# Attention of a mixed kernel: chunks of 64 tokens, two sequences in the halves of the partitions, state carried from pair to pair

## The chip, the core and the metric

The kernel runs on one core of one Trainium2 chip. A core has a matrix engine (TensorE, PE in the profile, with the loading of its weights shown as PEld), a vector engine (VectorE, DVE), an activation engine (ScalarE, ACT), a general engine (GpSimd, POOL) and a queue that issues most transfers (SyncE, SP). Data lie in an on-chip memory of 128 partitions; PE writes to eight banks of its own accumulation memory, 128 partitions by 512 numbers of 32 bits each, and ACT and DVE read them out. The metric is the time of one execution in microseconds (us). All numbers are 32-bit floats.

## The reference

Two blocks in a row. The first is a chunked state-space attention over 4 sequences, 8 heads, 768 tokens, head width 32 and state width 16. The chunk length is free to choose, since the chunked form gives the same numbers for any length:

```python
cum = np.cumsum(la, axis=-1)                    # la = log of the decays a, in one chunk
L = np.exp(cum[:, :, :, None] - cum[:, :, None, :]) * causal
M = np.einsum('bhin,bhjn->bhij', Cc, Bc) * L
y = einsum('bhij,bhjd->bhid', M, xc) + einsum('bhin,bhnd->bhid', Cc, state) * np.exp(cum)
state = exp(sum(la)) * state + sum over j of (Bc[j] x xc[j]) * np.exp(cum[-1] - cum[j])
```

Its output, 3072 tokens of 256 numbers, goes through the second block: four branches e with two layers each, weighted by normalized probabilities p:

```python
for e in range(4):                              # w1: 256 x 1024, w2: 1024 x 256
    out += p[:, e:e+1] * (np.maximum(x @ w1[e], 0.0) @ w2[e])
```

## The kernel before, in words

**The branches.** Tokens are taken in four blocks of 768; a block has three pairs of 256 columns (`yT`, one value of kind V per pair, features in the partitions and tokens in the columns). The matrix products of both layers are made by a fast scheme of sums and products (20 products instead of 24 per group of four feature blocks); each product is `product` (L1017), two matmuls of 128x128 weights with 256 columns, and stands in the trace as four records. DVE and POOL make the sums of weights (L1077), of tokens (L1147) and of results (L1044, L1357), DVE the gates (L1052), and ACT moves banks to memory and back (L1026, L1031, L1317). Weight sums of the first block are stored and read again by the later blocks.

**The attention before.** A chunk is 128 tokens of one sequence; chunks go round the four sequences, so that chunk c follows on chunk c - 4. For each chunk:

- transfers (`fetch`): the tokens and heads `xb`; the running sums of the log decays, spread over all partitions, `ab` (512 KB); the same sums per head, `ah`.
- `decays`: the matrix L of each head in `MT`, 128x128. It is made by ACT (`decay`, eight exponentials per chunk, L525) and cut to the causal half by POOL (`causal`, L535), or, in the first chunks and in chunks 2 and 4 (`SCANS`), by DVE as a scan along the columns (`scan`, L518) into a buffer of its own, `LT0`. `fade` (L544, L885) puts B times the last column of L beside it, as 16 more columns of MT.
- `score` (L501): four matmuls of 32 rows, 128 columns of weights and 256 columns. DVE multiplies the result into MT (L940).
- `outputs`: the carried state times the query, four matmuls on 32x32 pieces of the array (L963), where neighbouring chunks turn the output by some quarters of the partitions; and `inner` (L550), eight matmuls of 128 rows, 32 columns of weights and 144 columns: 128 for the output and 16 for the new state.
- `carry`: ACT takes the 16 columns out (L560), DVE transposes them and adds the old state times its decay (L994, L996).

Two chunks are a pair of 256 columns. Scores are made for two chunks in a burst, outputs for two or four.

**What sets the order.** Up to about 13 us the instructions stand as written (the opening): loads, identity and masks, logs and their sums by PE (`sum_logs`), probabilities (`turn_gates`, `spread_gate`), chunks 0 and 1 with decays by the scan (`spread` on PE, L665, then `scan`), and half of the first product (`first_half`, L697). Everything after goes through a planner (`Plan`): PE's order is the list `line`; the other engines' work is placed by due times that follow from it, with durations and a start time written into the code. Buffers of each kind are given out by it. `PAIRS_AT` says at which step of which unit the scores and outputs of the next block's chunks enter the list. SP issues the transfers in the planner's order. The end of the last block (`last`) turns results with PE (L1431), copies them out and stores each with one transfer (`send`, L1435); the blocks before it store through `leave` (L1411).

The kernel names its planned costs; those that the change touches, as they are before:

```python
pe(.66 * len(cs), lambda e: score(
pe(.93 + .49 * len(cs) if cs[0] >= NSEQ else .4 + .49 * len(cs), fn, reads=reads, ...
now, START = 13.0, 12.1
```

Of the kernel before, what the change touches and what calls it, by code (L numbers as in the profile page):

```python
# [35 lines left out]
SCORED, OWN, LEAD, LEFT = 7, 4, 5, 3  # L36
SCANS = 2, 4
FILLED, EARLY, FADE = 3, 4, "POOL"
CUT = {(c, 0): "DVE" for c in range(2, 6)}
HORIZON, OPENING, LOADED = 26.0, 80.0, 0.5  # L40
ORDERS = (0, 1, 2, 3), (3, 1, 2, 0), (0, 1, 2, 3), (3, 1, 2, 0)
PAIRS_AT = ((1, 22, "s0"), (2, 1, "o0"), (2, 1, "s1"), (2, 24, "s2"), (3, 0, "o12")), (
    (1, 1, "s0"), (1, 24, "s1"), (2, 0, "o01"), (2, 24, "s2"), (3, 1, "o2"))
# [316 lines left out]
def kernel(  # L360
# [17 lines left out]
    HN = P  # L378
    T = NCH * P
    OB, OBT, OCT = DM, DM + HN, DM + 2 * HN  # L380
# [6 lines left out]
    SPREAD = 3  # L387
# [3 lines left out]
    assert NSEQ == E == EPB == 4 and sum(b.n for b in blocks) == NCH  # L391

    def real(c):
        return c % NSEQ * NC + c // NSEQ

    def turn_of(c):

        return (0, 2, 1, 3)[c % NSEQ]

    def turned(c):  # L400

        lo = P // NQ * turn_of(c) if c >= NSEQ else 0
        return [(lo, 0, P - lo), (0, P - lo, lo)][:1 + (lo > 0)]
# [5 lines left out]
    acut_d = tc.dram_tile([NCH, NH, P], FP32, name="acut_d")  # L409
    cum_d = tc.dram_tile([NCH, NH, P], FP32, name="cum_d")  # L410
    p_d = tc.dram_tile([E, NCH, P], FP32, name="p_d")
# [9 lines left out]
    def some(n, shape, name, pool=const):  # L421
# [3 lines left out]
        "V": some(NV - 4, [P, 2, FB], "v"),  # L425
        "W": some(NW, [P, 2 * FB], "w"),
        "bank": some(8, [P, 512], "bank", psum),
        "xb": some(4, [P, W], "xb"),
        "ab": some(4, [P, NH * P], "ab"),
        "ah": some(3, [HN, P], "ah"),  # L430
        "MT": some(2, [P, 2, NH, P + N], "MT"),
        "ctm": some(4, [HN, NT, P], "ctm"),
        "cts": some(4, [HN, NT, P], "cts"),
        "dec": some(8, [HN, P], "dec"),
        "A": some(4, [P, NT, N], "A"),
        "S": some(10, [HN, D], "S"),
        "gate": some(2, [P, max(b.n for b in blocks), P], "gate"),
        "Y": some(12, [P, FB], "Y"),
        "cum": some(2, [NCH * NH // 2, 2, P], "cum"),
        "neg": some(1, [P, 2, NCH * NH // 2], "neg"),  # L440
        "dram": [None, None, None],
    }
    LT0 = const.tile([P, 2, NH, P], FP32, name="LT0")
    homes["V"][:0] = [
        LT0[:, j, h:h + NQ].rearrange("p (a h) s -> p a (h s)", a=2)
        for j in range(2) for h in range(0, NH, NQ)]
    st = {c: {} for c in range(NCH)}
# [4 lines left out]
    def load_tokens(c, xb):  # L452
        src = xbc[real(c)]
        if len(turned(c)) > 1:
            nc.sync.dma_start(out=xb[:, :OBT], in_=src[:, :OBT])
            for there, here, n in turned(c):
                nc.sync.dma_start(out=xb[here:here + n, OBT:], in_=src[there:there + n, OBT:])
        else:
            nc.sync.dma_start(out=xb, in_=src)

    def load_decays(c, ab):
        nc.sync.dma_start(
            out=ab, in_=(acut_d if c in SCANS else cum_d)[real(c)].rearrange("h s -> (h s)").partition_broadcast(P))

    def load_heads(c, ah):
        src = cum_d[real(c)].unsqueeze(1).to_broadcast([NH, N, P])
        for there, here, n in turned(c):
            nc.sync.dma_start(out=ah[here:here + n], in_=src[there // N:(there + n) // N])
# [23 lines left out]
    def mask(c, ctm, xb):  # L492
        for t in range(NT):
            nc.scalar.mul(ctm[:, t], xb[:, OCT:OCT + P], tmask[:, t:t + 1])  # L494

    def score(cs, ctm, xb, banks, order=range(4)):
        views = [b.rearrange("p (c t s) -> p c t s", c=2, t=NT) for b in banks]
        for j, c in enumerate(cs):
            for r in order:
                k = slice(32 * r, 32 * r + 32)  # L500
                nc.tensor.matmul(  # L501
                    out=views[r][:, j], lhsT=xb[j][k, OBT:OBT + P],
                    rhs=ctm[j][k].rearrange("p t s -> p (t s)"),
                    start=(j == 0), stop=True, tile_position=(32 * r, 0),
                    skip_group_check=True)

    def quarter(c, r):

        q = (r + (turn_of(c - c % 2) if c >= NSEQ else 0)) % NQ
        return slice(NT * q, NT * q + NT)  # L510

    def place(c, h):

        return (h + NH // 2) % NH if c >= NSEQ and c % 2 else h

    def scan(LT, src, lo):
        w = src.shape[1]
        nc.vector.tensor_tensor_scan(  # L518
            out=LT.rearrange("p h s -> p (h s)")[:, lo:lo + w], data0=src,
            data1=ident.rearrange("p h s -> p (h s)")[:, :w], initial=0.0,  # L520
            op0=ALU.mult, op1=ALU.add)

    def decay(c, MT, ab, neg, h):

        nc.scalar.activation(  # L525
            out=MT[:, place(c, h), 0:P], in_=ab[:, h * P:h * P + P], func=AF.Exp,
            bias=neg[:, h % NT, NQ * real(c) + h // NT:NQ * real(c) + h // NT + 1])

    def causal(e, MT, h, n):
        if e == "DVE":  # L530
            nc.vector.tensor_tensor(
                out=MT[:, h:h + n, 0:P], in0=MT[:, h:h + n, 0:P],
# [1026 lines left out]
    for c in (4, 5):  # L1559
        carry(c)  # L1560
# [152 lines left out]
```

## Time and profile before

| | us |
|---|---|
| median of 3 runs | 609.67 (609.55 to 609.75) |
| the profiled execution's own time | 609.86 |
| its span, first to last instruction | 608.1 |
| PE busy | 602.0 |
| DVE busy | 490.5 |
| ACT busy | 296.0 |
| POOL busy | 159.3 |
| transfers | 99.78 MB, 164 GB/s over the span |
| granted clock of PE | 1.00 |

A group of the profile is one line of the code on one engine with one shape. For a matmul, `32*128 32x256` means weights of 32 rows and 128 columns, and 256 columns streamed over 32 rows. The busy time of a group does not count the overlap with the instruction before it, so a mean of 380 ns with a busy time of 384.3 us for 1636 records is no contradiction: records overlap. `<-` names what ended the idle time before a group. In a timeline the first column is the start, the second the time from the first start to the last end of the merged instructions.

### The profile page before, as it was taken

What the parts mean: (1) busy time and instruction counts of PE and PEld (TensorE: products, weight loads), DVE (VectorE), ACT (ScalarE), POOL (GpSimd) and SP (SyncE); (2) the same over time, 40 slices, a digit from 0 to 9 for tenths busy, and PEclk for the clock granted to TensorE, in tenths of its full rate; (3) what the DMA queues carried; (4) which work ended last, traced back from release to release, by engine and by line L of the source; (5) the groups of instructions that cost most, each with busy time, mean ns of one, the idle gap of its engine ahead of it and who ended that gap; (6) DMA issues with size and microseconds to landing.
All of it is one profiled execution on the core that took longest, in us unless ns stands there. A gap on an engine that the chain in (4) does not pass through costs nothing.

```text
span 608.1 us, 10074 instructions
## 1 busy us (share of the span) xinstructions
PE 602.0 (99%) x3381; PEld 515.1 (85%) x3381; DVE 490.5 (81%) x842; ACT 296.0 (49%) x698; POOL 159.3 (26%) x208
## 2 busy tenths in 40 slices
PE   8999999999999999999999999999999999999997
PEld 5778878888888888888888888888888888888886
DVE  7779999999989894777879988396785989576695
ACT  5567475488443328948251334734444242434441
POOL 7565664646451002776400100200000000000000
PEclk9999999999999999999999999999999999999999
DMA  7968569786924239982432324962241322974001
GB/s 219 280 202 270 164 208 329 258 286 218 319 83 116 61 71 330 286 288 106 138 96 87 113 33 144 326 199 90 70 138 63 110 72 35 331 227 143 1 0 53
DMA packets 88564, 99.78 MB, mean 164 GB/s; under 512 B 26932, under 2 KB 54208, under 8 KB 88512
## 3 DMA queue, kind: packets, MB, share of 16 engines
q1 hardware_dynamic: 88356, 99.08, 52.3%
q8 instruction: 27, 0.44, 0.3%
q14 instruction: 25, 0.20, 0.1%
q10 hardware_dynamic: 156, 0.06, 0.0%
HBM read 78.93 MB, written 20.17 MB: 163 GB/s over the span
## 4 chain that ended last, share of the span: by engine, by line
PE 97%; DVE 1%; DMA 0%; ACT 0%; issue 0%; SPq 0%; DVEq 0%
PE bank L1017 91%; PE bank L550 2%; PE bank L501 2%; PE bank L963 1%; PE bank L690 1%; PE bank L665 0%; DMA w<-in_w_dram 0%; DVE bank L1175 0%; PE bank L1494 0%; DVE v L1044 0%; PE bank L1431 0%; DVE v L1052 0%; ACT A L560 0%; PE bank L697 0%; PE bank L655 0%
## 5 line engine op out<-in xcount | busy, mean ns | idle before, releaser
L1017 PE MATMUL bank<-v,w 128*128 128x256 f32 x1636 | 384.3, 380 | 0.3 <-DVE v L1044 0.2
L1017 PEld LDWEIGHTS bank<-v,w 128*128 128x128 f32 x1636 | 309.4, 190 | 45.8 <-issue 2.2
L1017 PE MATMUL bank<-Y,w 128*128 128x256 f32 x692 | 177.1, 381 | 0.6 <-ACT LT L978 0.4
L1317 ACT COPY v<-bank 128x512 f32<-128x512 f32 x105 | 61.5, 586 | 184.4 <-PE bank L1017 183.0
L1017 PEld LDWEIGHTS bank<-Y,w 128*128 128x128 f32 x692 | 130.6, 190 | 21.1 <-ACT v L1026 0.9
L1044 DVE TENSOR_TENSOR v<-v,v 128x512 f32<-128x512 f32 x183 | 136.3, 760 | 2.3 <-ACT v L1026 0.9
L1052 DVE SCALAR_TENSOR_TENSOR v<-bank,gate 128x512 f32<-128x512 f32 x145 | 99.5, 687 | 43.6 <-PE bank L1017 40.4
L1077 POOL TENSOR_TENSOR w<-w,w 128x512 f32<-128x512 f32 (+1 forms) x77 | 84.7, 1109 | 49.5 <-DVE v L1044 19.2
L1175 DVE TENSOR_TENSOR bank<-bank,v 128x512 f32<-128x512 f32 x82 | 55.9, 695 | 34.5 <-PE bank L1017 17.9
L1026 ACT COPY v<-bank 128x512 f32<-128x512 f32 x99 | 58.0, 586 | 49.0 <-PE bank L1017 39.0
L1031 ACT COPY bank<-v 128x512 f32<-128x512 f32 x122 | 70.5, 592 | 9.0 <-DVE v L1052 3.9
L1017 PE MATMUL bank<-LT,w 128*128 128x256 f32 x232 | 58.4, 380 | 0.0
L525 ACT ACTIVATE MT<-ab,neg 128x128 f32<-128x128 f32 x160 | 50.6, 392 | 4.9 <-DMA ab<-cum_d 4.9
L1017 PEld LDWEIGHTS bank<-LT,w 128*128 128x128 f32 x232 | 43.9, 190 | 6.4 <-issue 0.6
L535 POOL TENSOR_SCALAR_AFFINE_SELECT MT<-MT 128x512 f32<-128x512 f32 x38 | 24.6, 653 | 74.5 <-ACT MT L525 54.6
L1044 DVE TENSOR_TENSOR v<-bank,v 128x512 f32<-128x512 f32 x27 | 18.6, 688 | 9.0 <-PE bank L1017 7.4
L1357 DVE TENSOR_TENSOR v<-v,v 128x256 f32<-128x256 f32 x63 | 24.0, 420 | 0.9 <-ACT v L1317 0.7
L940 DVE TENSOR_TENSOR MT<-bank,MT 128x512 f32<-128x512 f32 x36 | 22.8, 682 | 1.6 <-POOL w L1077 1.2
L1044 POOL TENSOR_TENSOR v<-v,v 128x512 f32<-128x512 f32 x7 | 8.9, 1272 | 44.3 <-DVE v L1044 44.3
L1052 DVE SCALAR_TENSOR_TENSOR v<-v,gate 128x512 f32<-128x512 f32 x27 | 19.2, 710 | 0.4
L1317 ACT COPY LT<-bank 128x512 f32<-128x512 f32 x15 | 8.8, 584 | 17.2 <-PE bank L1017 17.2
L494 ACT ACTIVATE ctm<-xb,tmask 128x128 f32<-128x128 f32 x48 | 15.9, 390 | 1.0 <-DMA xb<-in_xbc_dram 0.9
(121 smaller groups left out, 322.9 us busy)
## 6 DMA issues: line engine op xcount, KB each, us to landing
w<-w_d SPq DMA_DIRECT2D x128, 256.0 KB
w<-in_w_dram SPq DMA_DIRECT2D x72, 256.0 KB
w_d<-w SPq DMA_DIRECT2D x64, 256.0 KB
ab<-cum_d SPq DMA_DIRECT2D x20, 512.0 KB
gate<-p_d SPq DMA_DIRECT2D x15, 384.0 KB
xb<-in_xbc_dram SPq DMA_DIRECT2D x17, 192.0 KB
out_dram<-v SPq DMA_DIRECT2D x144, 16.0 KB
xb<-in_xbc_dram SPq DMA_DIRECT2D x7, 320.0 KB
```

The source lines that it names most:

```text
L525: nc.scalar.activation(out=MT[:, place(c, h), 0:P], in_=ab[:, h * P:h * P + P], func=AF.Exp, bias=neg[:, h % NT, NQ * real(c) + h // NT:NQ ...
L535: nc.gpsimd.affine_select(out=MT[:, h:h + n, 0:P], in_=MT[:, h:h + n, 0:P], compare_op=ALU.is_ge, fill=0.0, base=0, pattern=[[0, n], [1, P ...
L940: nc.vector.tensor_mul(to, g, to)
L1017: nc.tensor.matmul(out=o, lhsT=w[:, j], rhs=x if half is None else x[:, j], start=(start and j == 0), stop=(j == 1), skip_group_check=True)
L1026: act(.5, lambda e: nc.scalar.copy(out=flat(v), in_=bank.t), reads=[bank], writes=[v])
L1031: act(.54 if to - lo > FB else .32, lambda e: nc.scalar.copy(out=bank.t[:, lo:to], in_=flat(v)[:, lo:to]), reads=[v], writes=[bank])
L1044: plan.add(engines, lambda e: (on(e).tensor_add if sign > 0 else on(e).tensor_sub)(flat(v), whole(x), whole(y)), reads=[x, y], writes=[v], ...
L1052: dve(D512, lambda e: nc.vector.scalar_tensor_tensor(out=h.t, in0=whole(x).rearrange("p (j m) -> p j m", j=JJ), scalar=0.0, in1=g.t[:, 2 * ...
L1077: (on(e).tensor_add if sign > 0 else on(e).tensor_sub)(out, x, y)
L1175: dve(D512, lambda e: (nc.vector.tensor_add if sign > 0 else nc.vector.tensor_sub)(to.t, bank.t, whole(x)), reads=[x, bank], writes=[to])
L1317: act(.5, lambda e: nc.scalar.copy(out=flat(v), in_=bank.t), reads=[bank], writes=[v], hold=HOLD)
L1357: plan.add(engines, lambda e: (on(e).tensor_add if sign > 0 else on(e).tensor_sub)(o[1](), x[1](), y[1]()), reads=[v for v in vs if v is n ...
```

## The change

A chunk becomes 64 tokens. A pair is now the 64-token chunks of all four sequences at the same place, 256 columns as before, so there are twelve pairs, and pair p follows on pair p - 1. Sequences 0 and 1 lie in partitions 0 to 63 of the decay matrices, 2 and 3 in 64 to 127; s is the half, c the place within it, z = 2s + c the sequence.

- L per head and sequence is 64x64; `MT` is 128 x (4, 2, 2, 64). `decay` makes 16 exponentials of 64 columns per pair, `causal` is DVE's minimum with a bound, over 512 columns, twice per pair; pairs 0 and 1 use the scan. `LT0`, `SCANS`, `CUT`, `FADE` and `acut_d` are gone.
- `score`: sixteen matmuls per pair, 32 rows, 64 columns of weights, 128 columns. `scores` takes one pair or two.
- `outputs`: sixteen matmuls of state times query (32x32, 128 columns), 32 of `inner` (64 rows, 32 columns of weights, 64 columns), and sixteen of a new function `state` (64 rows, 32 columns of weights, 64 columns) with the decayed B in a buffer `F` of its own. The new state comes out with its rows in place, so DVE's transpose goes; `carry` takes the two heads of a quarter with masks.
- `unturn` takes the second half's output back to its quarters with ACT.
- Transfers: tokens `xt` (two per pair), heads `bct` (one per two pairs, 512 KB), `ab` in four issues and 512 KB per pair, `ah` in four issues per pair from a second copy of the sums, `cumh_d`.
- The opening makes pair 0 (one set of four scans, one inner stage) and the spread of pair 1; the first product is left to the planner. All four first weights are loaded ahead of pair 1's tokens.
- `leave` and `last` store by the new order of tokens; a `send` of `last` is two transfers, one per half of the partitions.
- `PAIRS_AT` and the planner's costs are written for the pairs.

In the built program PE has 2263 matmuls in place of 1698, DVE 851 instructions for 842, ACT 641 for 699, POOL 141 for 208, SP 559 for 548.

```diff
-PAIRS_AT = ((1, 22, "s0"), (2, 1, "o0"), (2, 1, "s1"), (2, 24, "s2"), (3, 0, "o12")), (
-    (1, 1, "s0"), (1, 24, "s1"), (2, 0, "o01"), (2, 24, "s2"), (3, 1, "o2"))
+PAIRS_AT = (
+    ((1, 22, "s", 3, 4), (2, 1, "o", 3), (2, 14, "o", 4), (2, 24, "s", 5, 6), (3, 1, "o", 5)),
+    ((1, 1, "o", 6), (1, 24, "s", 7, 8), (2, 1, "o", 7), (2, 20, "o", 8)),
+    ((0, 24, "s", 9, 10), (1, 24, "o", 9), (2, 1, "o", 10), (2, 24, "s", 11), (2, 36, "o", 11)))
...
+    def score(p, ctm, bct, banks, half=0):
+        e = p % 2
+        for c in range(2):
+            lo = FB * half + P * c
+            for s in range(2):
+                for r in range(NQ):
+                    k, to = slice(32 * r, 32 * r + 32), slice(HALF * s, HALF * s + HALF)
+                    nc.tensor.matmul(
+                        out=banks[r][to, lo:lo + P].rearrange("p (t i) -> p t i", t=NT),
+                        lhsT=bct[k, 2 * s + c, 0, HALF * e:HALF * e + HALF],
+                        rhs=ctm[k, :, 2 * s + c],
+                        start=(c == 0 and not half), stop=True, tile_position=(32 * r, HALF * s),
+                        skip_group_check=True)
...
+    def inner(q, t, z, to, y, xt, MT, start):
+        s, c = divmod(z, 2)
+        k, h = slice(HALF * s, HALF * s + HALF), (NQ * t + q) * D
+        nc.tensor.matmul(
+            out=y[to:to + 32], lhsT=xt[k, c, h:h + D], rhs=MT[k, q, c, t], start=start, stop=True,
+            tile_position=(HALF * s, to), skip_group_check=True)
+
+    def state(F, xt, banks, at):
+        for c in range(2):
+            for r in range(NQ):
+                for s in range(2):
+                    k = slice(HALF * s, HALF * s + HALF)
+                    nc.tensor.matmul(
+                        out=banks[s][32 * r:32 * r + 32, at + c * NT * D:at + (c + 1) * NT * D].rearrange(
+                            "p (t d) -> p t d", t=NT),
+                        lhsT=F[k, r, c],
+                        rhs=xt[k, c, :DM].rearrange("p (t q d) -> p t q d", t=NT, q=NQ)[:, :, r],
+                        start=False, stop=True, tile_position=(HALF * s, 32 * r),
+                        skip_group_check=True)
...
+        pe(1.7 if goes_on else 1.45, fn, reads=reads, writes=ys)
...
         def send(d, n, r, to):
-            c = blocks[k].first + 2 * n
-            dma(lambda e: nc.sync.dma_start(
-                out=dst[d, c // NSEQ][:, c % NSEQ + to.start:c % NSEQ + to.stop],
-                in_=r.t[:, 0, to.start * P:to.stop * P].rearrange("p (q m) -> p q m", m=P)),
-                kb=64 * (to.stop - to.start), reads=[r])
+            dma(lambda e: [nc.sync.dma_start(
+                out=dst[d, 3 * k + n, c][:, to],
+                in_=r.t[HALF * c:HALF * c + HALF, 0, to.start * P:to.stop * P].rearrange(
+                    "p (s m) -> p s m", m=P)) for c in range(2)],
+                2, kb=64 * (to.stop - to.start), reads=[r])
```

## The prediction

> **What bounds the kernel now.** I read the page's busy table first, then the groups of TensorE (PE), then PE's timeline around three attention bursts, its waits, and at last the first 15 us and the last 10 us.
>
> ```profile
> PE 602.0 (99%) x3381; PEld 515.1 (85%) x3381; DVE 490.5 (81%) x842; ACT 296.0 (49%) x698; POOL 159.3 (26%) x208
> ...
> PE 97%; DVE 1%; DMA 0%; ACT 0%; issue 0%; SPq 0%; DVEq 0%
> ```
>
> The groups by line and shape, of PE alone (count of records, busy us, mean ns of one, idle before):
>
> ```profile
> L1017 PE MATMUL bank<-v,w 128*128 128x256 f32 x1636 | 384.3, 380 | 0.3 <-DVE v L1044 0.2
> ...
> L501 PE MATMUL bank<-ctm,xb 32*128 32x256 f32 x192 | 14.2, 400 | 0.0
> L550 PE MATMUL bank<-MT,xb 128*32 128x144 f32 x320 | 11.7, 289 | 0.4 <-DMA w<-in_w_dram 0.4
> L963 PE MATMUL bank<-cts,S 32*32 32x256 f32 x160 | 4.8, 386 | 0.0
> ```
>
> PE is busy for 99% of the span and makes 97% of the chain that ended last, and no PE wait of 1 us stands in the list of waits. So time is won or lost mostly by what PE must issue. The trace has two records per matmul written in the code. A product's records (L1017) start 0.2155 us apart, so 380 ns is a latency, not a price. Attention is the three other lines; their price is read from the timeline of PE, as what a burst adds to the products' pace:
>
> ```profile
> 66.83 0.81 PE L1017 MATMUL bank<-v,w 128*128 128x256 f32 x3
> 67.58 1.15 PE L501 MATMUL bank<-ctm,xb 32*128 32x256 f32 x16
> 68.65 0.70 PE L1017 MATMUL bank<-Y,w 128*128 128x256 f32 x2
> ...
> 116.47 0.38 PE L1017 MATMUL bank<-Y,w 128*128 128x256 f32 x1
> 116.78 0.71 PE L963 MATMUL bank<-cts,S 32*32 32x256 f32 x32
> 117.42 2.18 PE L550 MATMUL bank<-MT,xb 128*32 128x144 f32 x64
> 119.54 0.92 PE L1017 MATMUL bank<-LT,w 128*128 128x256 f32 x3
> ```
>
> The reader is to see that 32 records of L963 take 0.71 us, hardly more than one record's own 0.39: matmuls on different 32x32 pieces of the array run side by side, and the trace has their starts 6.7 ns apart. The last product before the scores starts at 67.27, the second one behind them at 68.97: 1.705 us, less two products, is **1.27 us per score burst**. In it are four rounds of 256 columns (0.862), and 0.41 at the edges: 0.093 to drain the products, 0.104 for the first 128 columns of weights, 0.02 until the fourth tile starts, 0.088 to drain, 0.104 for the products' weights.
>
> **The bursts on PE.** The sum is against the profiled execution, 609.86 us (span 608.1 and 1.76 around it), 0.19 above the median of the three runs, 609.67. Products are the same: 1284 of 256 columns instead of 1280 and eight of 128.
>
> Before: eleven score bursts behind the opening, 11 x 1.274 = 14.0 us; eight output bursts whose excesses in the timeline are 1.32, 1.91, 1.62, 2.96, 2.96, 1.91, 2.85 and 1.80, in sum 17.3 (the third without its scores and 0.6 of waiting). Together 31.3.
>
> After, scores: a pair has 32 records on eight tiles of 32x64, 128 columns each. A round of 256 columns takes 0.2155, so one of 128 about 0.109; four rounds are 0.436. Edges: 0.093 + 0.053 (64 columns of weights) + 0.047 (eight starts of 6.7 ns) + 0.192 = 0.385. Three bursts of one pair and four of two: 3 x 0.82 + 4 x 1.26 = 7.5.
>
> After, outputs of a pair: 32 records of state times query (four rounds of 128 columns, 0.436), 64 inner records of 64 columns on eight tiles of 64x32 (eight rounds of 0.0556, half of 0.109 with the fixed 2 ns kept, 0.445), and 32 records of the new state product, four such rounds, 0.222. Edges: in 0.118, from 32x32 to 64x32 tiles 0.113, starts 0.094, out 0.192. That is 1.62, and 1.40 for the last pair, which has no state: 10 x 1.62 + 1.40 = 17.6. Together 25.1: **6.2 us less**. No row shows a round of 64 columns on eight tiles. Eight starts of 6.7 ns fill 0.0536 of its 0.0556, so that is the lowest. The highest is the pace that the long inner burst holds, 0.0306 us per record (64 records in 2.18, less one's 0.29); I take the low end, since the L963 row has 32 starts within some 0.33 us, 10 ns each, nearer to it.
>
> **The opening.** Before, the first product of all weights W0 is complete at 14.66, where full products begin. After, chunk 0's and 1's tokens are one pair: 4 scans (0.67 each) instead of 8, one inner stage instead of two. But more stands ahead of it in ACT's and PE's order: the scores need both halves of the heads, twice 256 KB in place of twice 128 KB, so I put them at 6.3 where before has 5.70. From scores to inner before takes 3.98 us (5.70 to 9.68), through ACT's copies, the logs and the spread of the next pair, which PE issues ahead of inner; the gate copy is now 512 wide (0.59 by the 128x512 rows of ACT, for 0.26). So inner is at 10.6, its data out at 11.3, the copy for the products done at 11.7, and W0's eight records (1.72) end at 13.5: **1.2 us less**. Ends: 2.1 less if the heads land no later and ACT's copy is covered, 0.4 less if they are a microsecond late.
>
> **The tail.** Each of the last stores becomes two, one per half of the partitions.
>
> ```profile
> 604.54 1.42 SPq L1435 DMA_DIRECT2D out_dram<-v  x3
> ```
>
> ```profile
> 604.58 0.29 DVE L1499 COPY v<-bank 128x128 f32<-128x128 f32 x1 [1.06 <-PE bank L1494]
> ```
>
> The last data are copied by 604.87, yet SP issues the last store only at 605.54: it is already the queue, 0.47 us per issue, that ends the kernel. Four sends from 603.55 on are eight issues: 0.89 (what that one took) and seven of 0.475 end at 607.8 instead of 605.96; without that long one at 607.4. **1.6 us more**, ends 1.0 and 2.0. A smaller store is no cheaper to issue: the 16 KB stores of L1411 have a median of 0.43.
>
> **What lies beside PE.** The masks on DVE go from 36 of 512 columns (0.68) and 21 of 256 to 46 of 256 (0.36 apart): 14 us less; scans 5 less; the causal cut moves from POOL to DVE, 18 more of 0.67, 12 more; fades on DVE 14 of about 0.3, 4 more; carry about even (30 small operations for 36). Six 512-wide weight sums leave DVE for POOL, 6 less. DVE ends near 482 of 490 us, and is covered by PE; from 60 to 160 us it is busy for 95.0 of 100, so there the cover is thin, and each microsecond more on it would be a wait of PE for a sum or a gate. ACT's 160 decays have half the columns. On SP, decays and carried heads are four issues each per pair (some 0.4 to 0.65), about 559 in all for 548; the broadcast of decays halves, from 21 x 512 KB to 10. No charge while POOL and SP keep their idle time; without it, R2. New is the order: the state of a pair waits for the pair before (PE, two ACT copies, three DVE operations, then PE), where before four chunks were independent. PAIRS_AT puts ten or more product steps between outputs later, but in the first 35 us only some six; behind a late output the next products queue on PE, and the token sums wait for its copies.
>
> Sum: -6.2 - 1.2 + 1.6 = -5.8, so **604.0 us**.
>
> **Rivals.**
> R1, rounds of 64 columns cost as much as those of 128, since weights (32 columns, 0.025 by the drain into L963) or the sequencer don't keep up: 11 x 8 + 10 x 4 rounds of 0.053 more are 6.8, giving 610.8, no measurable change. Against it: weights of 32 columns are shorter than the round.
>
> R2, the plan waits: the state's chain in the first 35 us, or DVE between 60 and 160. For it: before has 2.7 us of such small stalls already, most between 40 and 55 us, and 0.9 within bursts. As much again gives 607.5.
>
> R3, slower: short matmuls have a floor and do not start closer than 30 ns, the pace that the inner burst holds over 64 records. 1728 records x 0.0306 are 52.9 and edges 7.6, against 31.3: 29 more, 633 to 639. By my sum a record costs 10 ns in the mean (17.5 of rounds over 1728); from 13.5 ns on (5.8 / 1728 more) the change loses. Against it: 6.7 ns between starts in the L963 burst, and its row. The Trainium skill, "TensorE: Matmul & The Clock Gate", section "Wait — 56ns, not 53.3ns?", says that start-to-start never drops below about 25 ns however small N is; by that the records alone would be 43 us and the whole some 624 us (an estimate), but this trace's 6.7 ns between tiles disagrees, so that floor can at most hold within one tile.
>
> R4, better: the opening gains 2.1 and the tail costs 1.0, and PE's stalls of 40 to 55 us shrink with DVE's load: 601 to 602.
>
> **Numbers.** Forecast (602.3 to 606) 0.48, R4 0.17, R2 0.18 (a quarter of it past the old time), R1 0.06, R3 0.05, other losses 0.06. A measurement here can tell 0.2%, 1.2 us. Faster: 0.48 + 0.17 + 0.14 + 0.03 = 0.82; same 0.05; slower 0.13. The range holds the forecast, R4 and most of R2: 600.0 to 609.0.
>
> **What would show it.** The two output kinds of rows, inner and state: 96 records within some 0.9 us, starts near 7 ns; score bursts with 0.82 and 1.26 of excess; first full product near 11.8; the last store's issue over 2 us behind the last copy. Wrong would be: inner rounds of 0.1 us (R1, R3), PE waits for DVE or ACT rows of the carry before outputs 1 to 3 (R2), or a first product past 13 us.

## The result, and the profile after

The changed kernel takes 650.8 us (median of four runs, 649.3 to 651.8) beside 609.7 us of the kernel before on the same chip: 1.067 times as long, with a 95% interval of 1.065 to 1.069. The forecast was 604.0 with a range up to 609; it is wrong by 47 us and in sign. The profiled execution has a span of 649.4 us.

From the page of the changed kernel: busy times, the clock that PE was granted in 40 equal slices of the span, and the chain that ended last, by engine and by line.

```profile
PE 611.4 (94%) x4508; PEld 522.7 (80%) x4508; DVE 492.8 (76%) x851; ACT 281.8 (43%) x640; POOL 136.6 (21%) x141
...
PEclk7888979969999999999999999999999999999999
...
PE 86%; DMA 5%; SPq 5%; DVE 2%; issue 1%; ACT 0%; POOL 0%; DVEq 0%; ACTq 0%; POOLq 0%
```

PE's busy time has grown by 9 us, the span by 41. The chain, 97% PE before, is now PE for 86%, and 10% of it, some 65 us, are transfers and SP's queue. The clock is below 0.9 in six of the first nine slices (146 us); before it was 1.00 throughout. What PE waited for (total, times, longest):

```profile
PE bank L973 <- DVE v L1008: 10.8, 1, 10.8
PE bank L906 <- DVE MT L683: 5.3, 1, 5.3
PE bank L973 <- ACT v L1277: 4.0, 1, 4.0
```

L973 is the product, L906 the state times the query; two waits of 3 us for POOL follow. Each wait names an engine, but none of these engines was short of time: by the windows below DVE's busy time between 60 and 160 us fell by 19. They waited themselves. The timeline of DVE around the opening has one case; its bracket gives the idle time before the row and what ended it:

```profile
5.60 2.44 DVE L505 TENSOR_TENSOR_SCAN MT<-bank,identr 128x256 f32<-128x256 f32 x4 [0.86 <-PE bank L665]
15.82 0.46 DVE L528 TENSOR_TENSOR F<-xt,MT 128x64 f32<-128x64 f32 x2 [7.79 <-DMA xt<-in_xbc_dram]
```

The scans are done at 8.0, and then DVE stands still for 7.8 us until the tokens `xt` of pair 0 land. Pieces of the chain of the first 160 us (start, length):

```profile
19.02 8.18 DMA cum_d<-cum
...
36.09 10.64 DMA xt<-in_xbc_dram
...
76.94 6.20 DMA ah<-cumh_d
...
130.22 10.63 DMA xt<-in_xbc_dram
...
141.08 0.70 DVE v L1008
```

A store of the sums, issued at 19.02, is done 8.2 us later, and a load of tokens takes 10.6. The three longest waits of PE lie behind such pieces: the one of 5.3 us ends at 49.8, behind the tokens of 36.09; the one of 4.0 at 84.7, behind the carried sums `ah` of 76.94; and the longest, of 10.8, at 141.8, behind the tokens of 130.22: DVE's next step, at 140.87, made the decayed B (`F`) from them, and the gate that PE needed (L1008) stood behind it. The stretches of both kernels, before and then after (the first column the window, then PE, PEld, DVE, ACT, POOL busy; at the end granted clock, share of the 16 transfer engines, GB/s):

```profile
0.00:14.00 14.00, 12.44 (x100) 7.67 (x101) 10.29 (x30) 7.40 (x22) 9.86 (x27) 1.00 0.68 212
14.00:60.00 46.00, 45.50 (x294) 36.12 (x293) 38.12 (x73) 30.22 (x90) 27.73 (x41) 1.00 0.80 251
60.00:160.00 100.00, 99.56 (x615) 85.16 (x614) 94.98 (x142) 62.54 (x170) 56.28 (x63) 1.00 0.78 256
```

```profile
0.00:14.00 14.00, 10.77 (x80) 4.95 (x80) 4.91 (x18) 5.25 (x12) 4.85 (x16) 0.81 0.46 139
14.00:60.00 46.00, 34.84 (x530) 27.94 (x524) 24.00 (x47) 15.50 (x46) 24.32 (x32) 0.83 0.53 155
60.00:160.00 100.00, 83.76 (x834) 69.09 (x832) 76.00 (x125) 51.48 (x148) 44.69 (x40) 0.91 0.61 191
```

From 160 to 300 us PE is full again, 140.00 of 140. In the first 160 us PE is busy for 129.4 us in place of 157.5, and yet the transfer engines are less busy than before, 0.46 to 0.61 for 0.68 to 0.80. So transfers are late although the engines that carry them have time. That is the question for the runs: why.

The single packets of the trace answer it in part. A load of 192 KB for one half-pair of tokens (`xt`, L441) makes 128 packets of 1536 bytes. I added up their durations and divided by the time from the first to the last of a group of loads: 2.0 packets are under way at a time in the mean, between 1.8 and 2.04 in each of the eleven groups; 256 packets take about 9 us. Before, the 1536-byte packets of the opening had 13 under way, those of the later loads 3.4 to 8.9 in the mean. One packet takes 0.071 us, no longer than before (0.078). That is what a load on two of the sixteen engines would show. The source of this transfer has as its outermost dimension the two sequences, `[2, 64, 384]`; the kernel before reads 128 rows in a row.

### The profile page after: what moved, and what is told of

Read it like the earlier page. It is cut to its first block, busy times and chain, and to the rows that moved or that the text cites. A ratio compares the mean times of both kernels' runs of the same rounds, so it can differ in the third digit from the quotient of the medians.

```text
span 649.4 us, 12194 instructions
## 1 busy us (share of the span) xinstructions
PE 611.4 (94%) x4508; PEld 522.7 (80%) x4508; DVE 492.8 (76%) x851; ACT 281.8 (43%) x640; POOL 136.6 (21%) x141
## 4 chain that ended last, share of the span: by engine, by line
PE 86%; DMA 5%; SPq 5%; DVE 2%; issue 1%; ACT 0%; POOL 0%; DVEq 0%; ACTq 0%; POOLq 0%
PE bank L973 82%; DMA xt<-in_xbc_dram 3%; SPq L460 2%; DMA cum_d<-cum 1%; PE bank L536 1%; PE bank L906 1%; SPq L441 1%; SPq L468 1%; DMA ah<-cumh_d 1%; PE bank L497 0%; PE bank L545 0%; SPq L746 0%; SPq L452 0%; DVE MT L683 0%; DVE v L1008 0%
## 5 line engine op out<-in xcount | busy, mean ns | idle before, releaser
L973 PE MATMUL bank<-v,w 128*128 128x256 f32 x1876 | 440.8, 383 | 16.6 <-DVE v L1008 10.8
L973 PEld LDWEIGHTS bank<-v,w 128*128 128x128 f32 x1876 | 358.2, 192 | 70.0 <-DVE v L1008 12.0
L973 PE MATMUL bank<-Y,w 128*128 128x256 f32 x692 | 177.5, 381 | 0.4 <-DVE Y L1103 0.4
L1000 DVE TENSOR_TENSOR v<-v,v 128x512 f32<-128x512 f32 x242 | 174.7, 745 | 1.7
L1273 ACT COPY v<-bank 128x512 f32<-128x512 f32 x120 | 70.4, 586 | 200.0 <-PE bank L973 190.4
L1008 DVE SCALAR_TENSOR_TENSOR v<-bank,gate 128x512 f32<-128x512 f32 x162 | 111.3, 687 | 50.5 <-PE bank L973 48.0
L973 PEld LDWEIGHTS bank<-Y,w 128*128 128x128 f32 x692 | 130.9, 190 | 20.1 <-issue 0.9
L982 ACT COPY v<-bank 128x512 f32<-128x512 f32 x111 | 65.3, 588 | 50.3 <-PE bank L973 41.2
L513 ACT ACTIVATE MT<-ab,neg 128x64 f32<-128x64 f32 x160 | 40.8, 340 | 11.1 <-DMA ab<-cum_d 11.1
L518 DVE TENSOR_TENSOR MT<-MT,bound 128x512 f32<-128x512 f32 x20 | 16.4, 834 | 9.8 <-ACT MT L513 9.8
L868 POOL TENSOR_TENSOR cts<-ctm,dec 128x512 f32<-128x512 f32 x11 | 14.2, 1295 | 39.9 <-DVE v L1008 18.2
L1008 DVE SCALAR_TENSOR_TENSOR v<-v,gate 128x512 f32<-128x512 f32 x30 | 22.2, 741 | 0.4
L925 ACT COPY v<-bank 64x256 f32<-64x256 f32 (+1 forms) x33 | 12.3, 374 | 14.9 <-PE bank L545 14.7
L683 DVE TENSOR_TENSOR MT<-bank,MT 128x256 f32<-128x256 f32 x46 | 16.3, 415 | 0.0
L906 PE MATMUL bank<-cts,S 32*32 32x128 f32 x352 | 8.4, 300 | 8.1 <-DVE MT L683 5.3
```

The source lines that it names most:

```text
L513: nc.scalar.activation(out=MT[:, q, c, t], in_=ab[:, c, h], func=AF.Exp, bias=neg[:, e, t, i:i + 1])
L518: nc.vector.tensor_tensor(out=v, in0=v, in1=bound.unsqueeze(1).to_broadcast([P, 4 * n, HALF]), op=ALU.min)
L973: nc.tensor.matmul(out=o, lhsT=w[:, j], rhs=x if half is None else x[:, j], start=(start and j == 0), stop=(j == 1), skip_group_check=True)
L982: act(.5, lambda e: nc.scalar.copy(out=flat(v), in_=bank.t), reads=[bank], writes=[v])
L1000: plan.add(engines, lambda e: (on(e).tensor_add if sign > 0 else on(e).tensor_sub)(flat(v), whole(x), whole(y)), reads=[x, y], writes=[v], ...
L1008: dve(D512, lambda e: nc.vector.scalar_tensor_tensor(out=h.t, in0=whole(x).rearrange("p (j m) -> p j m", j=JJ), scalar=0.0, in1=g.t[:, 2 * ...
```

## The experiments

Theory A: the waits come from these loads, which use two engines and hold up whatever stands behind them on those two. Theory B: they come from the new order, the serial chain of states, the planner's due times and the opening, and transfers are late as a consequence.

**Loads split.** The whole change is kept, and each load is issued as two, one sequence of 64 rows each:

```diff
-        nc.sync.dma_start(out=xt[:, c], in_=src[c, k, e][:, :, :OBT])
+        for s in range(2):
+            nc.sync.dma_start(out=xt[HALF * s:HALF * s + HALF, c], in_=src[c, k, e][s][:, :OBT])
```

> The changed kernel with each load of a pair's tokens (192 KB, two sequences times 64 rows in one issue) made as two issues, one sequence of 64 rows each; the plan is the same, SP gets one issue more per load. Theory A (these loads run on two of the sixteen DMA engines, as the 1536-byte packets with a mean concurrency of 2.0 show, and everything behind them on those two comes late): the packets' concurrency goes well past 2, the DVE idle of 18.9 us behind the tokens and the PE waits of 10.8, 5.3 and 4.0 us go, the granted clock is near 1.00, and the time is about 611 us, within 607 to 615: the 609.9 of the profiled execution of the kernel before, less 3.0 for the bursts as the changed kernel's own timeline has them (28.3 for 31.3), plus 3.1 for the tail (6.7 for 3.6 us behind PE's end), plus about 1 for the opening. Theory B (the waits come from the new order itself: the state carried from pair to pair, the due times of the plan, the opening): the waits in the first 60 us stay, and the time is 630 us or more.

Measured: 617.7 us, 1.013 of before (1.012 to 1.015). That is 33.1 us of the 41.1. It lies 2.7 above the range that I had given theory A, 607 to 615, and 12 below theory B's 630. The stretches:

```profile
0.00:14.00 14.00, 10.02 (x65) 4.91 (x66) 6.04 (x22) 5.10 (x12) 8.86 (x25) 0.78 0.62 184
14.00:60.00 46.00, 44.51 (x594) 35.17 (x593) 36.77 (x61) 26.65 (x78) 24.99 (x27) 0.96 0.69 198
60.00:160.00 100.00, 99.31 (x933) 85.22 (x932) 92.63 (x151) 59.06 (x163) 64.02 (x52) 1.00 0.78 243
```

PE is nearly full again from 14 us on, and no pause between products is longer than 1.2 us. The packets of `xt` now have 6 to 9 under way, and 256 of them take 2.5 to 3.8 us. SP's queue shows how a narrow load stops what is behind it: four loads of weights and the second pair's tokens, first in the changed kernel, then with the loads split.

```profile
4.95 6.51 SPq L468 DMA_DIRECT2D w<-in_w_dram  x4
11.50 4.44 SPq L441 DMA_DIRECT2D xt<-in_xbc_dram  x2
```

```profile
6.23 2.12 SPq L469 DMA_DIRECT2D w<-in_w_dram  x4
8.39 2.39 SPq L442 DMA_DIRECT2D xt<-in_xbc_dram  x4
```

The same four issues take 6.5 us behind two narrow loads and 2.1 behind four wide ones. Theory B alone is out; 8.3 us beyond before are left for it.

**Only the opening's loads split.** The condition `p > 1` keeps the one issue for the ten later pairs:

```diff
+        if p > 1:
+            nc.sync.dma_start(out=xt[:, c], in_=src[c, k, e][:, :, :OBT])
+            return
```

> The changed kernel with only the opening's four loads of tokens (pairs 0 and 1) split in two issues; the planned loads of the ten later pairs stay on two engines. If the late first data set the loss, most of the 33.1 us that the split won comes here and the time is below 630. If it is the planned loads, which keep two of the sixteen engines for 9 to 17 us each and hold up what is behind them, only the opening's part comes, 2.5 us by the first product (21.30 against 18.77) and at most 2 more: 646 to 649.

Measured: 642.7 us, 1.054 (1.052 to 1.056). The loads of the later pairs cost most, 25.0 us; the four of the opening are worth 8.1, more than the 2.5 to 4.5 that I gave them. I had taken little more than the first product's delay for them, 2.4 us in the traces. SP's later issues moved by more: the second four loads of weights start at 16.24 in place of 20.95. That this makes up the rest is likely, but not shown.

**The same fault put into the kernel before.** From chunk 2 on the token part of each load is read as two interleaved halves, so that the outermost dimension of the source is 2. The tokens of a chunk come in another order than the reference's; amount and work are the same. Where the heads came with the tokens in one transfer, they now have one of their own.

```diff
-        if len(turned(c)) > 1:
-            nc.sync.dma_start(out=xb[:, :OBT], in_=src[:, :OBT])
-            for there, here, n in turned(c):
-                nc.sync.dma_start(out=xb[here:here + n, OBT:], in_=src[there:there + n, OBT:])
-        else:
-            nc.sync.dma_start(out=xb, in_=src)
+        nc.sync.dma_start(out=xb[:, :OBT], in_=src.rearrange("(j a) w -> a j w", a=2)[:, :, :OBT])
+        for there, here, n in turned(c):
+            nc.sync.dma_start(out=xb[here:here + n, OBT:], in_=src[there:there + n, OBT:])
```

> The kernel before, with the token part of each load from chunk 2 on read in two interleaved halves of 64 rows, so that the source's outermost dimension is 2 as in the changed kernel; the amount is the same, and the heads' part gets an issue of its own. The tokens of a chunk come in another order, so the output is not the reference's. Theory A: the mean concurrency of these packets falls from over 10 to 2, PE waits appear in the first 160 us with a lower granted clock, and the time is 8 to 45 us longer (the changed kernel's 650.8 less the 611 estimated without its two-engine loads would be 40, but here the tokens are a part of one chunk's load, and the two chunks of the opening keep theirs). Theory B: the transfers are covered as they were, and the time stays within 609 to 612.

Measured: 635.0 us, 1.042 (1.040 to 1.044), 25.6 us more. Behind the opening the packets run with 1.7 to 2.1 under way. PE's longest wait, a piece of the chain and the second stretch of this kernel:

```profile
PE bank L716 <- ACT v L783: 5.9, 1, 5.9
```

```profile
25.74 11.29 DMA xb<-in_xbc_dram
```

```profile
14.00:60.00 46.00, 37.75 (x235) 29.24 (x236) 24.47 (x53) 21.56 (x69) 19.11 (x33) 0.85 0.57 187
```

The kernel before, with nothing of the new order, shows the same picture: waits in the name of ACT or DVE, a lower clock, transfer engines at 0.57 in place of 0.80, and a load of tokens that takes 11.3 us in the chain. So it is shown from both sides that loads of this shape bring these waits, and cost 33 and 26 us. That just two engines carry such a load is read from the 2.0 packets.

**The tail alone, in the kernel before.**

```diff
-            dma(lambda e: nc.sync.dma_start(
-                out=dst[d, c // NSEQ][:, c % NSEQ + to.start:c % NSEQ + to.stop],
...
+            dma(lambda e: [nc.sync.dma_start(
+                out=dst[d, c // NSEQ][h:h + HALF, c % NSEQ + to.start:c % NSEQ + to.stop],
...
+                for h in (0, HALF)], kb=64 * (to.stop - to.start), reads=[r])
```

> The kernel before, with each store of the last block's end made as two transfers, one per half of the partitions; nothing else differs. The prediction's tail: 1.6 us more (1.0 to 2.0), so 610.7 to 611.7 beside 609.7. The changed kernel's trace has 3.1 us more between PE's end and the span's end; if that is the tail's own price and not an echo of the late transfers, the time is 612.4 to 613.2. A theory by which the second half's issue is covered gives no change.

Measured: 613.35 us, 1.0067 (1.0055 to 1.008): 3.9 us more, with 3.4 to 4.9 in the interval. The last stores on SP, of the kernel before and with the stores split:

```profile
598.62 7.33 SPq L1435 DMA_DIRECT2D out_dram<-v  x7
```

```profile
598.53 11.09 SPq L1435 DMA_DIRECT2D out_dram<-v  x14
```

PE's work ends at the same place (604.5). In the trace an issue of the whole store takes 0.40 us in the median and one of half the partitions 0.60, so SP is behind from the first store on.

**The second half of each last store on ACT's queue**, from the split run:

```diff
-            dma(lambda e: [nc.sync.dma_start(
+            dma(lambda e: [(nc.sync, nc.scalar)[c].dma_start(
                 out=dst[d, 3 * k + n, c][:, to],
```

> As the run with split token loads, and of the last stores' two halves one is issued by SP and one by ACT's queue. If the tail is SP's queue of 14 issues of 0.6 us each, seven per queue end as they did in the kernel before, 3.6 us behind PE's end in place of 6.7, and the time falls by 3 us (2 to 3.5). If the stores' own transfers or their number set the end, or ACT's issues delay its copies, less than 1 us.

Measured: 615.9 us, 1.010 (1.009 to 1.012), 1.8 less than the split run. I had forecast 2 to 3.5. From PE's end to the span's end are 4.4 us, for 6.7, and 3.6 before. So SP's queue was most of the tail's 3.1; ACT's issues stand in the way of its own copies (one waits 0.49 behind an issue), which may be why not all of it returns.

**State ahead of inner in the output burst**, to see what sets PE's pace:

```diff
+            if goes_on:
+                state(s["F"].t, s["xt"].t, [y.t for y in ys], FB)
             for c in range(2):
                 for t in range(NT):
...
-            if goes_on:
-                state(s["F"].t, s["xt"].t, [y.t for y in ys], FB)
```

> As the run with split token loads, and in an output burst the 32 records of the state product stand ahead of the 64 inner records. In the changed kernel the 64-column records start 6.9 ns apart for the first 32 and about 8.25 ns apart from the 33rd on. Theory Q (PE's instructions are fetched ahead to a limited depth, and behind it the pace is the sequencer's): the state records, now first, start about 7 ns apart, the inner records behind them about 8.2 ns apart, and the excess of a burst stays at 1.85 to 1.95 us. Rival (the slow pace belongs to the inner records' form or to two rows of tiles that wait for one another): the pace is bound to the kind of record, not its place, the inner records keep a fast first half wherever they stand, and the excess moves by 0.05 us or more. The time stays within 1 us of the split loads' run in both.

Measured: 617.9 us, 1.014 (1.012 to 1.016), as the split run. The timeline of PE in one output burst, with loads split, and then with the state first:

```profile
125.82 0.80 PE L537 MATMUL bank<-MT,xt 64*32 64x64 f32 x60
...
126.47 0.51 PE L546 MATMUL bank<-xt,F 64*32 64x64 f32 x31
126.92 1.13 PE L974 MATMUL bank<-Y,w 128*128 128x256 f32 x4
```

```profile
126.02 0.45 PE L546 MATMUL bank<-xt,F 64*32 64x64 f32 x32
126.29 0.93 PE L537 MATMUL bank<-MT,xt 64*32 64x64 f32 x64
127.14 1.13 PE L974 MATMUL bank<-Y,w 128*128 128x256 f32 x4
```

By the single records, the 32 state records, now first, start 6.7 ns apart within each eight, 7.7 in the mean; in the split run the first 32 inner records do. The 64 behind them, whichever kind they are, come after a pause of 56 ns, then mostly by twos at 16.7 ns, 8.4 for each; a dozen or so stand alone in such a step, so the mean is 10.9 in the split run and 11.3 in this one. The burst adds 1.92 us in place of 1.89. So the pace goes with the place, not with the kind. The Trainium skill, "TensorE: Matmul & The Clock Gate", first table, gives PE a queue of 64 instructions; 32 records with their 32 weight loads are 64, so the trace agrees with the count. But no run here varied the queue, and one that is refilled at 8.4 ns while it is drained at 7.7 would hold out for more than 32 records, so what sets this pace is open.

**The opening in another order**, from the split run. With the loads wide, PE's opening still is late:

```profile
5.96 0.45 PE L498 MATMUL bank<-ctm,bct 32*64 32x128 f32 x8 [0.72 <-ACT ctm L488]
7.84 1.13 PE L498 MATMUL bank<-ctm,bct 32*64 32x128 f32 x24 [1.44 <-ACT ctm L488]
...
13.67 1.68 PE L666 MATMUL bank<-v,const-float32-1.0 32*64 32x256 f32 x16
15.28 2.06 PE L537 MATMUL bank<-MT,xt 64*32 64x64 f32 x58
...
18.76 5.42 PE L974 MATMUL bank<-v,w 128*128 128x256 f32 x24
```

The scores end at 9.0, but inner (L537) stands behind the spread of pair 1 (L666), and that behind the gates and the logs, whose steps go to and fro between ACT and PE. The edit takes gates and logs ahead of the scores, puts the spread behind them, gives DVE three of the four masks, and inner follows. In this run and in the one with both edits the decayed B is taken from the column after the masks in place of before them: the same operations on other data.

```diff
-    for zs in (slice(0, 2), slice(2, 4)):
-        mask(0, ctm[0], bct[0], zs)
+    next(turning)
+    mask(0, ctm[0], bct[0], slice(0, 2))
+    next(turning)
...
+    next(logs)
+    mask(0, ctm[0], bct[0], slice(2, 4))
     score(0, ctm[0], bct[0], seven)
...
+    next(gating)
+    spread(1, four, 1)
```

> As the run with split token loads, with the opening in another order: the gates are turned and the logs taken before the scores, the spread of pair 1 stands behind the scores, DVE masks three of the four quarters and POOL one, and pair 0's inner stage and state follow at once; the work is the same but for one copy made in two. In the split run the first full product starts at 18.76 us, behind an inner stage that PE starts at 15.28, though the scores end at 8.97. Theory O (the rest of the loss lies in the opening's order, chains of small steps ahead of inner in PE's and ACT's order): inner starts at 10 to 11, the first product at 12 to 13, and the time falls by 5 to 6.5 us, to 611 to 613. Rival (what the products need next, gates, decays and weights, comes no earlier): the products start earlier but wait in the next 50 us, and the time falls by less than 3 us.

Measured: 615.0 us, 1.008 (1.007 to 1.010), 2.7 less than the split run: the rival's number. In its profile, of an execution of 617.7 us, the longest of the five, inner starts at 13.19 and the first product at 16.25; inner now stood behind the second logs matmul.

**Opening and tail together:**

> Both of these edits together. By theory O and the tail as SP's queue the two gains add up: 8 to 9 us under the split run, 608.5 to 610, level with the kernel before or 0.1 to 0.2% under it. What is left then against the prediction's 604.0 is the bursts (3.2 us of the 6.2 that don't come, from the pace of 8.25 ns per record behind the first 32) and about 3 us of waits in the first 65 us and at 410. By the rivals 612 or more.

Measured: 613.1 us, 1.0056 (1.0044 to 1.007), 4.6 less than the split run, the sum of 2.7 and 1.8, not the 8 that I had hoped for. In its profile the first product starts at 14.99.

**Three tries to get the rest of the opening.** First, the decayed B ahead of the masks, the logs matmul behind the state, and matmuls that compute nothing in PE's pauses:

```diff
+    for _ in range(4):
+        idle(four[0][:, FB:], 2)
     for q in range(NQ):
         scan(0, q, MT[0], four[q], 0)
```

> As the run with the reordered opening and the two queues at the tail (613.07), with four things put right in the opening: the decayed B is taken from the last column of L before the masks change it; the second matmul of the logs stands behind the state product, so that inner no longer waits for it at 12.09 or 10.64; and nine matmuls of 256 columns that compute nothing stand where PE had nothing to do, since in that run inner and state took 2.6 us in place of 1.0, with a granted clock of 0.88 over the first 14 us. If the order of small steps is what held inner, it starts at 10.5 to 11, the first full product at 12.3 to 13 (14.99 there), the clock is above 0.95 over the first 14 us, and the time falls by 2 to 2.7 us to 610.3 to 611. If the gain is given back in waits of the next 50 us, it stays within 1 us of 613.

Measured: 617.3 us, 1.012 (1.010 to 1.014): a step back, by two faults of the edit. The scans read the bank that the idle matmuls write, so they waited for them and started at 8.33 in place of 5.35. And the store of the sums, which needs the logs matmul that I had put behind the state, was issued at 17.08 in place of 12.15; PE then waits 1.7 us for the carried sums of pair 1. The first product starts at 17.37. The clock, though, was 1.00 over the first 14 us, for 0.88.

The second is the planner with another start time; it also counts two issues for each load of tokens:

```diff
-    now, START = 9.6, 9.6
+    now, START = 12.0, 12.0
```

> As that run, and the planner starts its times at 12.0 in place of 9.6 and counts two issues for each load of tokens. The planner then works with the start that the trace shows, and the order of DVE, ACT, POOL and SP changes. If the waits of PE between 35 and 110 us (4.1 us in the split run, 2.2 in the kernel before) come from orders planned for another start, they fall by 1 to 2 us and the time is 608.5 to 610; if they come from the amount of work on DVE and the transfers there, the time stays within 0.6 us.

Measured: 621.3 us, 1.019 (1.017 to 1.021), 4.0 us worse. Neither number fits; some waits lie elsewhere than in that run (1.5 us at 96, 0.7 at 79), so the planned order is sensitive to it by some microseconds, and a truer start is not a better one.

The third has the idle matmuls behind the scans and in another bank, the logs' copy ahead of the spread, and inner behind the logs matmul again:

```diff
-    for _ in range(4):
-        idle(four[0][:, FB:], 2)
...
+    for _ in range(4):
+        idle(seven[0][:, FB:], 2)
...
+    next(logs)
+    aside(0, seven[0], 0)
     next(gating)
     spread(1, four, 1)
-    nc.sync.dma_start(out=p_d, in_=p_sb)
+    next(logs)
```

> As the run with the reordered opening and two queues at the tail (613.07), with the decayed B taken ahead of the masks and two faults of the later tries mended: the matmuls that compute nothing (six of 256 columns) stand in a bank that no scan reads, since there the four scans waited for them and came 3.0 us later (8.33 for 5.35); and the logs' copy by ACT is ahead of the spread of pair 1, so that the second logs matmul and the store of the sums come before inner. By theory O inner starts at 10.5 to 11.3, the first full product at 12.2 to 13, and the time is 610 to 611; no more, since the bursts (28.8) and the tail (4.4) stay. If something else takes the time back (the gate, the sums on the way to the decays of pair 2, the loads), the first product still moves, but the time stays above 612.

Measured: 612.9 us, 1.0057 (1.0043 to 1.007), as with both edits. Rows of PE and one of SP:

```profile
11.73 1.25 PE L537 MATMUL bank<-MT,xt 64*32 64x64 f32 x58
...
14.04 7.14 PE L981 MATMUL bank<-v,w 128*128 128x256 f32 x32
...
27.34 0.67 PE L914 MATMUL bank<-cts,S 32*32 32x128 f32 x32 [1.88 <-POOL cts L876]
```

```profile
19.37 3.88 SPq L461 DMA_DIRECT2D ah<-cumh_d  x4
```

The first product comes 4.7 us earlier than in the split run, though not at the 12.2 to 13 that I expected, and the time of the run with only the tail (615.9) falls by 3.0. 1.9 of it went into one wait: the state times query of pair 1 needs the carried sums, and SP issues their four loads only from 19.37 to 23.25, behind four loads of weights and four of decays. So I put these four loads ahead of the decays:

```diff
         load_w2(fb, homes["W"][4 + fb])
+    load_carried(1, homes["ah"][0])
```

> As the last run (612.89; first product 14.04), with the four loads of pair 1's carried sums issued by SP right behind the first weights, ahead of the four broadcasts of pair 2's decays; the planner orders what follows anew. In the last run PE waited 1.9 us at 27.35 for the product of query and decay of pair 1, whose sums SP had issued only from 19.37 to 23.25, and had 0.9 more in the second output burst. If SP's queue is what took the opening's gain back, those waits go and the time falls by 1.5 to 3 us, to 610 to 611.4. If another load that now comes later takes their place (the decays of pair 2, the tokens or the weights of the second block), it stays within 0.8 us of 612.9.

Measured: 615.2 us, 1.008 (1.007 to 1.010), 2.3 worse. The wait of 1.9 is gone, the first output burst starts at 25.04, and new waits came with the new plan: 0.6 and 1.2 in the scores of pair 2, and 1.9 at 111.7. I had expected a gain, or no change within 0.8.

```profile
31.16 0.85 PE L498 MATMUL bank<-ctm,bct 32*64 32x128 f32 x28 [1.19 <-ACT A L556]
```

No version here is faster than the kernel before; the best, at 612.9 to 613.1, is 0.6% above it.

## Why the prediction was wrong

Four terms can be set beside the split run, in which the narrow loads are gone (span 616.1 against 608.1, 8.0 more). I read them from the starts of PE's records: the first product with its eight records, what the bursts add, the pauses between products, and the time from PE's end to the span's end.

| | predicted | split run against before |
|---|---|---|
| opening, first product complete | -1.2 | +5.8 (18.76 + 1.72, against 14.66) |
| bursts, without waits | -6.2 | -3.0 (28.3 against 31.3) |
| waits in and between bursts | 0 | +2.1 (7.6 against 5.5) |
| tail | +1.6 | +3.1 (6.7 against 3.6) |
| sum | -5.8 | +8.0 |

- **The step that failed** is "what lies beside PE". It counted SP's issues ("about 559 in all for 548") and said "no charge while POOL and SP keep their idle time"; the loads of tokens have no line in it at all. I had costed a transfer by its bytes and its issue, and the bytes had not grown (94.3 MB for 99.8). How many engines carry it I did not ask. The split run and the narrow loads in the kernel before show 33.1 and 25.6 us for this alone. The Trainium skill, "DMA: Bandwidth & Descriptors", section "Why a DMA increments its semaphore by 16 and not by 1", says that a transfer uses the largest number of engines up to 16 that divides the outermost dimension (of a size above 1) of both sides. By it the change's load has two; the 2.0 packets under way agree, and the sentence would have given the sign. By the rows the term would have been 256 packets of 0.07 us on two engines, some 9 us for each pair, with all that is queued on these two behind it.
- **R2, the plan waits**, named the right symptom with the wrong source and size. Waits for DVE and ACT did come, 10.8 us the longest, but not from the chain of states or DVE's load: before the three longest the engines named waited for transfers, and DVE between 60 and 160 had 24 us free. With the loads split, a small part of R2 is left: PE waits for DVE 2.8 us in all, in place of 0.4 before. R2's 607.5 took only as much again as the small stalls of before.
- **The bursts.** Scores are as worked out: 0.821 for one pair (0.82) and 1.334 for two (1.26). Outputs are 1.893 in place of 1.62, the last 1.582 in place of 1.40: 2.9 us in eleven bursts. The rounds of the first 32 records have the predicted 0.056; the 64 behind them take 10.9 ns each where 7.0 were worked out, and these 0.25 us are nearly all of the difference. "I take the low end" was right for a third of the records. R3's floor of 30 ns is disproved: 96 records on tiles of 64x32 start within 0.95 us, 10 ns each. (Its sums are off as well: the edges listed add up to 8.4, not 7.6, and the 624 of the floor of 25 leaves the edges out; with them it is some 630.) The 25 ns of the Trainium skill, "TensorE: Matmul & The Clock Gate", section "Wait — 56ns, not 53.3ns?", don't hold across tiles either, by these records.
- **The opening** was worked out as 3.98 us from scores to inner, as before, with 0.33 more for the copy of the gates. It took 9.3 (5.96 to 15.28), 7.4 from the second part of the scores. PE waits 1.4 us for the heads' second half. Gates and logs stand between scores and inner as before, but ACT now takes the logs behind the gates' copy, at 10.45, where before it took them first, at 6.59. And PE, idle in between, was granted a clock of 0.78. Of the 7.0 us, reordering and filling the pauses moved the first product by 4.7 and the time by 3.0; 1.9 went into the wait for the carried sums.
- **The tail** was mis-sized: "a smaller store is no cheaper to issue" is true, but it is dearer, 0.60 us for 0.40. Fourteen of them gave +3.1 in the changed kernel and +3.9 alone, past my upper end of 2.0.
- **DVE** was to end near 482 us and has 492.8: the causal cut costs 0.83 in the mean where I took 0.67, 3 us in all, and the fades 0.52 where I took 0.3, again 3. What that cost in time no run here shows.
- **R1 and R4** don't arise: rounds of 64 columns are cheaper than those of 128 (0.056 and, at 8.4 ns for each record, 0.067, beside the 0.109 of my sum), and no gain in the opening came.

What stays open is how much of the remaining 8 us a plan made anew for the new opening would win; three tries moved the waits rather than removed them.

## What to carry to other kernels

When a change gives a transfer another shape, ask for its duration, not only for its bytes and its issue: here a source with an outermost dimension of 2 had 2.0 packets under way and took 9 us for 256 packets in place of some 3, and weights and sums queued behind it came late with it. A wait in the name of DVE or ACT is followed back until something is found that had no wait of its own; transfer engines that are less busy while transfers are late are a reason to look at how many of them each transfer uses. And a price for a burst is taken at the pace that holds over its whole length, not at the pace of its first 32 records.

## What the runs showed of the hardware

- One load of 128 rows of 1536 bytes with an outermost dimension of 2 has 2.0 packets under way; as two loads of 64 rows each, 6 to 9. Behind narrow loads even SP's issues of other, wide loads slow down: the four issues of weights in the opening take 6.5 us in place of 2.1, and one issue of a weight load elsewhere (L1028) 4.3 at most in place of 0.7.
- An issue of a store of 64 partitions takes SP 0.60 us, one of 128 partitions with twice the bytes 0.40.
- Matmuls of 64 columns on tiles of 64x32 start 7.7 ns apart in the mean for the first 32 records of a burst in the trace and 10.9 to 11.3 in the mean behind them, whichever kind comes first.
- With pauses in the first 14 us PE's granted clock was 0.78 (loads split) and 0.88 (opening and tail); with matmuls that compute nothing in the pauses 1.00, and the inner and state records then took 1.7 us (11.73 to 13.4) in place of 2.7 (11.65 to 14.33).
